# The first eight heads of an attention and feed-forward kernel: bias rows by products, wide exps, and casts on another engine

## The chip, the cores and the metric

The kernel runs on one core of one Trainium2 chip. A core has a matrix engine (TensorE, PE in the profile, with PEld for its weight loads), VectorE (DVE), ScalarE (ACT), GpSimd (POOL) and SyncE (SP). Each works through its own instructions in order, and semaphores let one wait for another. SP and POOL issue the DMA transfers of this kernel. SBUF holds the tiles; PSUM holds the results of products in 8 banks, each 128 partitions by 512 fp32 values. The metric is device time in microseconds (us), lower is better.

## The reference

Eight batches of eight heads, 576 positions of 64 values each, go through causal attention with a bias from running sums, and the result goes through a gated feed-forward block:

```python
scores = scale * np.matmul(q, k.transpose(0, 1, 3, 2))          # scale = 1/8
cum = np.cumsum(np.maximum(s, 0.0), axis=-1)
bias = -(cum[:, :, :, None] - cum[:, :, None, :])
scores = np.where(causal, -1e9, scores + np.minimum(bias, 0.0))
attn = softmax(scores)                                          # over the last axis
x = np.matmul(attn, v)  # (B, H, S, D) -> (B*S, H*D): 4608 x 512
out = (silu(x @ w_gate) * (x @ w_val)) @ w_out                  # 512 -> 1536 -> 512
```

Below the diagonal the bias is never positive, so the minimum needs no work of its own.

## The kernel before

Heads are handled in blocks of four (`hb`, 16 blocks; blocks 0 and 1 are batch 0). For a block, k and q are loaded as fp32 (`load_one`, L136), cast to bf16 (`cast_half` L248, `cast_one` L239), and transposed, for the early blocks by products with an identity on PE (`pe_transpose_half` L292, `pe_transpose` L281) into PSUM. `pe_out` (L305) copies the transposed halves out of PSUM into the tile `KQ`, nine groups of 128 columns in pieces of five and four, the upper and the lower 64 partitions into two tiles.

A tile `KQ[i][r]` holds 64 partitions of transposed q and k of two heads, and 64 partitions of bias rows, of which four are in use: the running sum split into a bf16 high and low part on one side (k or q), and constants 1 and -1 on the other. A product over all 128 partitions thus gives scores and bias together. The rest of the bias rows must be zero. The running sums are made by DVE into the tile `HL` (L200 to L232), one partition per head, and `aug` (L178) brings each head's four rows to its `KQ` tile with one small DMA per head.

`score_piece` (L338) makes the scores of one head in four pieces of at most 512 columns, each in one PSUM bank; two of them begin with a product that adds the causal mask (`lower`), in batch 0 only. ACT takes exp of each piece into the tile `pt`. So a head has three exps of 512 columns and one of 64. `av_piece` multiplies `pt` with v and a column of ones, `av_out` divides by the sum, `x_pe` (L439) transposes the result into `XT`, and the feed-forward block works from `XT` in tiles of 512 positions.

PSUM banks are handed out in Python by `take`, which takes the one that was given back first, and `give`. All order is written by hand: what stands first in the function is issued first on its engine. L905 to L976 are the opening that the change concerns: block 0 cast in halves by ACT and POOL, its transposes and bias rows, block 1 cast by DVE (L921), v of batch 0 cast by POOL (L924), the loads issued by POOL (v at L914, weights at L915 and L928, further k and q), the scores of heads 0 to 3 with block 1's transposes between them (`half_batch`, L891), heads 4 to 7, and `values`. `keep_warm` (L881) is products whose result nobody uses. After L976 the feed-forward work of one tile and the attention of the next batches are interleaved by a position counter (`pump`).

Of the kernel before, what the change touches and what calls it, by code (L numbers as in the profile page):

```python
# [19 lines left out]
def kernel(  # L20
# [11 lines left out]
    nc = tc.nc  # L32
# [73 lines left out]
    c8 = first.tile([BH, S], FP32)  # L106
    PTP = {0: first, "bufs": 7}
    lower = first.tile([128, 512], BF16)

    with tc.manual_schedule():  # L110
# [4 lines left out]
        bank = {i: psb.tile([128, 512], FP32, name=f"bank{i}") for i in range(8)}  # L115
# [4 lines left out]
        def take():  # L120
            b = min(bank, key=lambda x: released[x])
            assert released[b] < OPEN
            released[b] = OPEN
            return b
# [8 lines left out]
        def view16(b, w):  # L133
            return bank[b][:, 0 : w // 2].bitcast(BF16)
# [43 lines left out]
        def aug(hb, engs):  # L178
            for hh in range(HB):
                r, e = divmod(hh, 2)  # L180
                r0 = 64 * (1 - r)
                bh = hb * HB + hh
                engs[hh].dma_start(  # L183
                    KQ[hb % 2][r][r0 : r0 + 4, :, e * S : (e + 1) * S],
                    HL[bh : bh + 1, :, :, :],
                )
# [12 lines left out]
        nc.scalar.activation(warm, warm, AF.Exp)  # L199
        nc.vector.memset(HL[:, 0:2, 0, :].bitcast(FP32), ONES2)  # L200
# [6 lines left out]
        )  # L207

# [4 lines left out]
        for r in range(2):  # L213
            nc.gpsimd.memset(aug_rows(0, r)[:, 1, :], 0.0)
            nc.scalar.mul(
                KQ[0][r][64 * (1 - r) : 64 * (1 - r) + 64, 0, :],
                one_s[0:64, 0:1].to_broadcast([64, NR * S + 64]), 0.0,
            )
        pads(0)
        nc.vector.memset(aug_rows(1, 0), 0.0)  # L220
        for nm in ("k", "q"):
            load_one(1, nm, eng=nc.gpsimd)
        init_vt(0)
        pads(1)
# [67 lines left out]
        def pe_transpose_half(hb, name, g, r):  # L292
            j0, j1 = JG[g]
            if r == 0:
                bs = take()
                ps = view16(bs, (j1 - j0) * 128).rearrange("p (j x) -> p j x", x=128)
                tps[name, g] = [ps, bs, 2]
            ps = tps[name, g][0]
            ct = cts[name, hb]
            for j in range(j0, j1):  # L300
                nc.tensor.transpose(
                    ps[64 * r : 64 * r + 64, j - j0, :], ct[:, j, r, :], ident
                )
# [575 lines left out]
        spare = take()  # L879
# [5 lines left out]
        def row_half(nm, r, eng):  # L885
            for g in range(2):
                pe_transpose_half(0, nm, g, r)
            for g in range(2):
                pe_out(0, nm, g, r, eng)

        def half_batch(nm):  # L891
            for g in range(2):
                pe_transpose(1, nm, g)
                pe_out(1, nm, g, 0, nc.vector)

        def scores(h):
            for ci in range(4):
                score_piece(h, ci)
# [9 lines left out]
        aug(0, SP4)  # L908
        row_half("k", 0, nc.scalar)
        row_half("q", 0, nc.vector)  # L910
        cast_half(0, "k", 1, nc.scalar)
        cast_half(0, "q", 1, nc.gpsimd)
        nc.gpsimd.memset(aug_rows(1, 1), 0.0)
        load_v(0, range(5), nc.gpsimd)  # L914
        w_load("g", 0)  # L915
        aug(1, SP4)
        keep_warm(10)
        row_half("k", 1, nc.scalar)
        row_half("q", 1, nc.vector)
        keep_warm(10)  # L920
        cast_one(1, "k", nc.vector)  # L921
        cast_one(1, "q", nc.vector)
# [10 lines left out]
        scores(0)  # L933
        half_batch("k")
        scores(1)
        half_batch("q")
        scores(2)
        scores(3)
        for nm in ("k", "q"):
            for g in range(2):  # L940
                pe_out(1, nm, g, 1, nc.vector)
# [34 lines left out]
        give(spare)  # L976
# [88 lines left out]
```

## Time and profile before

| What | us |
|---|---|
| median of 3 runs | 375.78 (375.11 to 376.01) |
| the profiled execution | 375.79 |
| its span | 374.0 |
| PE busy | 360.7 |
| DVE busy | 289.6 |
| ACT busy | 240.4 |
| POOL busy | 212.3 |

The span runs from the first to the last instruction of one profiled execution, and all starts below count from its beginning. A row of the timeline has start, length, engine, line, operation, written tile <- read tiles, shapes, count, and in brackets the idle time of the engine ahead of it with what ended it. A row of the chain of waits has start, length and what the end waited for at that time. A group has busy time and mean length of one (ns). The granted TensorE clock was 0.999 in this execution.

### The profile page before, as it was taken

What the parts mean: (1) busy time and instruction counts of PE and PEld (TensorE: products, weight loads), DVE (VectorE), ACT (ScalarE), POOL (GpSimd) and SP (SyncE); (2) the same over time, 40 slices, a digit from 0 to 9 for tenths busy, and PEclk for the clock granted to TensorE, in tenths of its full rate; (3) what the DMA queues carried; (4) which work ended last, traced back from release to release, by engine and by line L of the source; (5) the groups of instructions that cost most, each with busy time, mean ns of one, the idle gap of its engine ahead of it and who ended that gap; (6) DMA issues with size and microseconds to landing.
All of it is one profiled execution on the core that took longest, in us unless ns stands there. A gap on an engine that the chain in (4) does not pass through costs nothing.

```text
span 374.0 us, 8759 instructions
## 1 busy us (share of the span) xinstructions
PE 360.7 (96%) x3259; PEld 230.6 (62%) x3300; DVE 289.6 (77%) x578; ACT 240.4 (64%) x471; POOL 212.3 (57%) x325
## 2 busy tenths in 40 slices
PE   7799899999999999999999999999999999999995
PEld 6584456655555556855685559655865585476464
DVE  8968776468995899588967997699858867975984
ACT  8777677698876877588757875686566523323321
POOL 8883555856455647494649464955675516315320
PEclk9999999999999999999999999999999999999999
DMA  7899999799877997896779675984132103002003
GB/s 239 193 258 253 219 257 267 237 303 247 245 186 220 254 262 196 178 281 205 211 167 266 178 182 174 255 206 98 40 119 62 35 19 128 2 0 95 20 0 114
DMA packets 97146, 64.23 MB, mean 172 GB/s; under 512 B 77232, under 2 KB 82736, under 8 KB 97104
## 3 DMA queue, kind: packets, MB, share of 16 engines
q1 hardware_dynamic: 84976, 41.46, 45.2%
q0 software_dynamic: 12128, 22.21, 22.6%
q8 instruction: 26, 0.43, 0.5%
q14 instruction: 16, 0.13, 0.1%
HBM read 37.90 MB, written 19.86 MB: 154 GB/s over the span
## 4 chain that ended last, share of the span: by engine, by line
PE 85%; DMA 6%; POOL 5%; ACT 1%; issue 1%; DVE 1%; DVEq 0%; POOLq 0%; ACTq 0%
PE bank L629 45%; PE bank L735 17%; PE bank L359 10%; PE bank L396 7%; PE bank L686 5%; DMA rawk<-in_k_dram 4%; DMA rawv<-in_v_dram 2%; POOL rawv L157 1%; POOL vt L168 1%; POOL wv L332 1%; ACT pt L369 1%; PE bank L287 0%; POOL rawq L140 0%; ACT kq L314 0%; POOL kq L211 0%
## 5 line engine op out<-in xcount | busy, mean ns | idle before, releaser
L369 ACT ACTIVATE pt<-bank 128x512 bf16<-128x512 f32 (+1 forms) x256 | 120.4, 510 | 31.0 <-PE bank L359 18.2
L629 PE MATMUL bank<-XT,wg 128*128 128x512 bf16 x418 | 110.3, 379 | 1.2 <-DVE pp L652 0.3
L629 PE MATMUL bank<-XT,wv 128*128 128x512 bf16 x412 | 109.3, 379 | 1.1
L650 ACT ACTIVATE th<-bank 128x512 bf16<-128x512 f32 x108 | 64.7, 599 | 55.9 <-PE bank L629 53.6
L652 DVE SCALAR_TENSOR_TENSOR pp<-th,bank 128x512 bf16<-128x512 bf16 x108 | 73.6, 682 | 19.2 <-ACT th L650 18.7
L663 DVE SCALAR_TENSOR_TENSOR ht<-pp,bank 128x512 bf16<-128x512 bf16 x108 | 74.1, 686 | 10.6 <-PE bank L629 0.4
L359 PE MATMUL bank<-kq 128*128 128x128 bf16 (+4 forms) x576 | 75.6, 240 | 1.5 <-DMA kq<-HL 1.0
L672 POOL TENSOR_TENSOR ht<-ht 128x512 bf16<-128x512 bf16 x35 | 40.4, 1154 | 52.2 <-DVE su L670 52.1
L359 PEld LDWEIGHTS <-kq 128*128 128x128 bf16 x576 | 45.8, 98 | 31.5 <-issue 1.9
L629 PEld LDWEIGHTS <-wv 128*128 128x128 bf16 x432 | 38.4, 98 | 36.5 <-issue 0.6
L629 PEld LDWEIGHTS <-wg 128*128 128x128 bf16 x432 | 38.3, 98 | 34.2 <-issue 0.7
L396 PEld LDWEIGHTS <-pt 128*128 128x128 bf16 x960 | 41.9, 98 | 17.2
L374 POOL TENSOR_SCALAR_AFFINE_SELECT pt<-pt 128x512 bf16<-128x512 bf16 x56 | 36.8, 658 | 27.3 <-ACT pt L369 22.7
L396 PE MATMUL bank<-vt,pt 128*128 128x65 bf16 x960 | 47.0, 194 | 0.4 <-POOL vt L168 0.3
L430 POOL DMA_DIRECT2D xs<-ot x24 | 21.7, 905 | 30.0 <-DVE ot L413 27.6
L735 PEld LDWEIGHTS <-ht 128*128 128x128 bf16 x336 | 31.2, 98 | 4.3
L413 DVE TENSOR_TENSOR ot<-bank,rc 128x320 bf16<-128x320 f32 x64 | 31.5, 492 | 2.2
L183 POOL DMA_DIRECT2D kq<-HL x48 | 28.9, 604 | 0.0
L735 PEld LDWEIGHTS <-su 128*128 128x128 bf16 x252 | 23.5, 98 | 3.3
L686 PE MATMUL bank<-wo,ht 128*128 128x512 bf16 x90 | 24.8, 379 | 0.3
L800 POOL TENSOR_TENSOR ysb<-ysb 128x512 f32<-128x512 f32 x12 | 15.2, 1270 | 15.3 <-DVE ysb L794 15.3
L379 POOL TENSOR_SCALAR_AFFINE_SELECT pt<-pt 128x64 bf16<-128x64 bf16 x56 | 14.8, 264 | 15.8 <-ACT pt L369 15.7
(93 smaller groups left out, 384.6 us busy)
## 6 DMA issues: line engine op xcount, KB each, us to landing
out_dram<-ysb POOLq DMA_DIRECT2D x32, 256.0 KB, 4.5
rawv<-in_v_dram SPq DMA_DIRECT2D x28, 256.0 KB
rawk<-in_k_dram SPq DMA_DIRECT2D x12, 576.0 KB
rawq<-in_q_dram SPq DMA_DIRECT2D x12, 576.0 KB
xs<-ot POOLq DMA_DIRECT2D x24, 160.0 KB, 3.5
ks<-ck SPq DMA_DIRECT2D x11, 288.0 KB
qs<-cq SPq DMA_DIRECT2D x11, 288.0 KB
rawk<-in_k_dram POOLq DMA_DIRECT2D x3, 576.0 KB, 7.3
```

The lines of the kernel that those rows point to most:

```text
L359: nc.tensor.matmul(sc[:, o : o + w], T[:, 1, e * S + 128 * tj : e * S + 128 * (tj + 1)], T[:, 0, e * S + lo : e * S + hi], start=not maske ...
L369: nc.scalar.activation(pt[:, c0 : c0 + n], sc, AF.Exp, scale=0.125)
L374: nc.gpsimd.affine_select(pt[:, 1088:1600], pt[:, 1088:1600], pattern=[[0, 4], [1, 128]], compare_op=ALU.is_ge, fill=zreg, base=0, channel ...
L396: nc.tensor.matmul(av[:, bi * (D + 1) : (bi + 1) * (D + 1)], pt[:, c0 : c0 + 128], VT[b % 2][:, tj, h, :], start=(tj == 0), stop=(tj == bi),)
L413: nc.vector.tensor_mul(ot[:, :, e * D : (e + 1) * D], av3[:, :, 0:D], rc[:, :, None].to_broadcast([128, NCH, D]),)
L629: nc.tensor.matmul(view(bs, TT), w[:, c, f0 : f0 + 128], xt[:, c, :], start=(c == 0), stop=(c == 3),)
L650: nc.scalar.activation(th, pg, AF.Tanh, scale=0.5)
L652: nc.vector.scalar_tensor_tensor(pp, in0=th, scalar=1.0, in1=pg, op0=ALU.add, op1=ALU.mult)
L663: nc.vector.scalar_tensor_tensor(hp[:, 2 * k2 : 2 * k2 + 2, :].rearrange("p a n -> p (a n)"), in0=pp, scalar=0.5, in1=pv, op0=ALU.mult, op ...
L672: (nc.vector if ft == NFT - 1 else nc.gpsimd).tensor_sub(hp[:, 1:3, :], hp[:, 1:4:2, :], hp[:, 0:3:2, :])
L686: nc.tensor.matmul(view(pys[ts_], DM), hps[ft // 2][:, 2 * (ft % 2) + half, c0 : c0 + 128], WO[j][:, ft % WKO, :], start=(ft == 0), stop=( ...
L735: nc.tensor.matmul(ps, lhs(p), rhs(p), start=(first and p == 0), stop=(last and p == NP - 1), skip_group_check=True,)
```

## The change

The eight banks become one PSUM tile, so that an instruction can cover two adjacent banks. For heads 0 and 1 the bias rows no longer come by DMA: a selection matrix (`sel`) in a product with `HL` puts the head's high and low part of the running sum on the right partitions of a pair of banks (`pick`), and ACT or DVE turns that into the k row and the q row with a scale and an offset per partition (`picked_row`). Heads 2 to 7 keep their DMAs. In batch 0, `wide_scores` makes a head's scores in two parts over a pair of banks, with exps of 1024 and 576 columns. The early transposes go to banks 0 to 2, which are kept for them, and each copy out covers nine groups (`early_out`), or four on ACT and five on DVE. The casts of block 0's second half (k) and of block 1 (k and q) go to POOL; the first load of v is issued ahead of them. Memsets are spread differently, and `keep_warm` has fewer products.

```diff
+    sel = first.tile([BH, 2, 2, 128], BF16)
...
-        bank = {i: psb.tile([128, 512], FP32, name=f"bank{i}") for i in range(8)}
+        banks = psb.tile([128, 8, 512], FP32, name="banks")
+        bank = {i: banks[:, i, :] for i in range(8)}
...
+        def take_pair():
+            b = min(range(7), key=lambda x: max(released[x], released[x + 1]))
+            assert max(released[b], released[b + 1]) < OPEN
+            released[b] = released[b + 1] = OPEN
             return b
...
+        for h in range(2):
+            for lo in range(2):
+                nc.vector.tensor_copy(
+                    sel[:, h, lo, 64 + lo : 68 : 2], ident[0:BH, h : h + 1].to_broadcast([BH, 2])
+                )
...
+        def early_transpose(hb, name, r=None):
             ct = cts[name, hb]
+            ps = early(name, 0, J)
+            for j in range(J):
+                if r is None:
+                    nc.tensor.transpose(ps[:, j, :], ct[:, j].rearrange("x r d -> x (r d)"), ident)
+                else:
+                    nc.tensor.transpose(ps[64 * r : 64 * r + 64, j, :], ct[:, j, r, :], ident)
...
+        for i in range(3):
+            released[i] = OPEN
+        spare = 7
...
+        def pick(h):
+            b = picked[h] = take_pair()
+            for lo in range(2):
+                for c0, c1 in ((0, 512), (512, S)):
+                    nc.tensor.matmul(
+                        banks[:, b + c0 // 512, 0 : c1 - c0], sel[:, h, lo, :],
+                        HL[:, lo, 1, c0:c1], start=(lo == 0), stop=(lo == 1),
...
+            if eng is nc.scalar:
+                nc.scalar.activation(dst, src_t, AF.Identity, bias=c[up, 0:1], scale=a[up, 0:1])
+            else:
+                eng.tensor_scalar(dst, src_t, a[up, :], c[up, :], ALU.mult, ALU.add)
...
+            b = take_pair()
+            order = ((1, 0), (2, 3))[part]
...
+            c0, n = CHUNK_PT[order[0]], (1024, 576)[part]
+            nc.scalar.activation(
+                pt[:, c0 : c0 + n],
+                banks.rearrange("p b n -> p (b n)")[:, b * 512 : b * 512 + n],
+                AF.Exp, scale=0.125,
+            )
...
-        aug(0, SP4)
-        row_half("k", 0, nc.scalar)
-        row_half("q", 0, nc.vector)
-        cast_half(0, "k", 1, nc.scalar)
+        aug(0, SP4, (2, 3))
+        aug(1, SP4)
+        early_transpose(0, "k", 0)
+        early_out(0, "k", 0, nc.scalar)
+        early_transpose(0, "q", 0)
+        pick(0)
+        load_v(0, range(1), nc.gpsimd)
+        cast_half(0, "k", 1, nc.gpsimd)
+        picked_row(0, 1, nc.scalar)
+        picked_row(0, 0, nc.vector)
+        picked_done(0)
+        early_out(0, "q", 0, nc.scalar, 0, 4)
+        early_out(0, "q", 0, nc.vector, 4, J)
+        pick(1)
+        early_transpose(0, "k", 1)
         cast_half(0, "q", 1, nc.gpsimd)
-        nc.gpsimd.memset(aug_rows(1, 1), 0.0)
-        load_v(0, range(5), nc.gpsimd)
+        for c in range(1, 5):
+            load_v(0, range(c, c + 1), nc.gpsimd)
+        picked_row(1, 1, nc.vector)
+        picked_row(1, 0, nc.vector)
+        picked_done(1)
+        keep_warm(4)
+        give(spare)
         w_load("g", 0)
-        aug(1, SP4)
-        keep_warm(10)
-        row_half("k", 1, nc.scalar)
-        row_half("q", 1, nc.vector)
-        keep_warm(10)
-        cast_one(1, "k", nc.vector)
-        cast_one(1, "q", nc.vector)
+        init_vt(0)
+        cast_one(1, "k", nc.gpsimd)
+        cast_one(1, "q", nc.gpsimd)
+        scores(0)
+        early_transpose(0, "q", 1)
+        early_out(0, "k", 1, nc.vector)
+        early_out(0, "q", 1, nc.scalar, 0, 4)
+        early_out(0, "q", 1, nc.vector, 4, J)
...
-        scores(0)
-        half_batch("k")
         scores(1)
-        half_batch("q")
-        scores(2)
+        early_transpose(1, "k")
+        early_out(1, "k", 0, nc.vector)
+        wide_scores(2, 0)
+        early_transpose(1, "q")
+        early_out(1, "q", 0, nc.scalar, 0, 4)
+        early_out(1, "q", 0, nc.vector, 4, J)
+        wide_scores(2, 1)
         scores(3)
-        for nm in ("k", "q"):
-            for g in range(2):
-                pe_out(1, nm, g, 1, nc.vector)
+        early_out(1, "k", 1, nc.vector)
+        early_out(1, "q", 1, nc.vector)
```

## The prediction

> **What bounds the kernel now.** The page comes first, for the size of the thing, then its chain of waits, to see which stretch is not plain TensorE work:
>
> ```profile
> span 374.0 us, 8759 instructions
> PE 360.7 (96%) x3259; PEld 230.6 (62%) x3300; DVE 289.6 (77%) x578; ACT 240.4 (64%) x471; POOL 212.3 (57%) x325
> PE 85%; DMA 6%; POOL 5%; ACT 1%; issue 1%; DVE 1%; DVEq 0%; POOLq 0%; ACTq 0%
> ...
> 22.81 15.78 DMA rawk<-in_k_dram
> 38.72 1.15 POOL ck L246
> ```
>
> PE carries the chain, and what is not PE lies ahead of 40 us: POOL's issues, then one load of k (head block 3) issued at 22.81 and landed at 38.60. The change touches only the work ahead of about 25 us, so I read that stretch in the timeline:
>
> ```profile
> 10.91 0.83 PE L359 MATMUL bank<-kq 128*128 128x128 bf16 x8 [0.99 <-DMA kq<-HL]
> 11.34 13.53 ACT L369 ACTIVATE pt<-bank 128x512 bf16<-128x512 f32 x32 [1.63 <-PE bank L359]
> 19.53 1.27 PE L396 MATMUL bank<-vt,pt 128*128 128x65 bf16 x30
> 23.42 0.44 PE L445 MATMUL bank<-ident,ot 128*128 128x128 bf16 x5
> 33.39 1.57 ACT L369 ACTIVATE pt<-bank 128x512 bf16<-128x512 f32 x3 [0.27 <-ACT th L650]
> 39.92 0.45 PE L287 MATMUL bank<-ident,ck 128*128 128x128 bf16 x5 [1.16 <-POOL ck L246]
> ...
> 9.51 4.89 POOL L157 DMA_DIRECT2D rawv<-in_v_dram x5
> 14.39 0.78 POOL L332 DMA_DIRECT2D wg<-in_moe_w_gate_dram x1
> 10.56 0.76 DVE L246 CAST ck<-rawk 128x1152 bf16<-128x1152 f32 x1
> 11.24 1.12 DVE L246 CAST cq<-rawq 128x1152 bf16<-128x1152 f32 x1
> 24.94 1.14 POOL L246 CAST ck<-rawk 128x1152 bf16<-128x1152 f32 x1 [1.36 <-DMA rawk<-in_k_dram]
> ```
>
> Head 0's scores wait at 10.91 for the bias row's DMA. Then 32 exps run almost without a hole, 1.69 us a head. Values of head 0 begin at 19.53, right after head 5's scores; the first transposes of attention output begin at 23.42. From there PE is packed (4.00 of 4.00 us busy in 28 to 32) until it idles 1.16 us for block 3's k. That wait is the only slack: work before it may come 1.16 us later for nothing, anything beyond goes into the end, since after 56 us no PE wait reaches the listing's threshold.
>
> Prices come from the groups by form:
>
> ```profile
> L369 ACT ACTIVATE pt<-bank 128x512 bf16<-128x512 f32 x24 | 12.6, 622 | 1.9 <-PE bank L359 1.6
> L369 ACT ACTIVATE pt<-bank 128x64 bf16<-128x64 f32 x8 | 2.2, 272 | 0.0
> L316 DVE COPY kq<-bank 64x640 bf16<-64x640 bf16 x7 | 5.7, 817 | 1.0 <-PE bank L287 0.7 <-PE bank L301 0.3
> L316 DVE COPY kq<-bank 64x512 bf16<-64x512 bf16 x7 | 5.0, 712 | 0.0
> L450 ACT COPY XT<-bank 128x576 bf16<-128x576 bf16 x2 | 1.3, 638 | 1.2 <-PE bank L445 1.2
> ```
>
> **The change, part by part.**
>
> *Wide exps.* A column costs (622-272)/448 = 0.78 ns, and three 512s in 1.57 us with the last at 0.60 make one step 0.485. So 1024 columns step in 0.90 (1.02 to the end) and 576 in 0.55 (0.67): 1.45 a head against some 1.6 now, 1.2 us over eight heads at most. Bounds of a head: 1.26 (columns alone) and 1.69 (today's pace). [...]
>
> *Head 0's rows.* ACT's two zeroings and two casts stand as now, and the nine k transposes end at 6.09. The copy of all nine, 64x1152 on ACT: 640 took 0.75, 512 took 0.72, 1216 from SBUF 1.21; I take 1.16, so 6.15 to 7.3. The ninth q transpose lies in that copy's bank and waits for it, and the picks are queued behind it on PE: one transpose (0.06), products of 512, 64, 512, 64 columns (0.216 a 512, from four in 1.03 with the last 0.38) and a tail of 0.2 end at 8.05. A product lies between 0.19 (64 columns) and 0.38. The added DVE work (memset, four tiny copies, three scalars: eight at 0.06, a memset, to 0.19, a reciprocal, so 0.5 to 1.5 us, less the removed 1.07 us memset) costs nothing: the bias low part ends at 6.83 now, and the picks wait until 7.36. Without that cover it would cost at most 0.4.
>
> From the picked pair ACT makes the k row, 64x576 (0.638 for XT's 576; bounds 0.6 and 1.21): 8.1 to 8.75. DVE's q row waits for ACT, as both read one pair: 0.72 (0.553 for a 576 scale in SBUF, 0.751 for two inputs), 8.8 to 9.55. DVE's half of the q copy waits for ACT's half (9.35) and follows, 0.82: 10.4. The k transposes of heads 2 and 3 wait for that copy on PE, and head 0's scores are queued behind them: 0.5, plus four warm products 0.25. Scores begin at 11.25, against 10.91. The DMA wait went; ACT, DVE and PE in a row took its place.
>
> [...]
>
> [...]
>
> *Heads 0 and 1.* A head's first part is 1536 columns, 0.65 and a tail, and its exp needs all of it: first exp at 12.1 (now 11.34). Exps: 12.1 to 13.0 and 13.0 to 13.55. Second part waits for DVE's rows of head 1 (two of 0.72 after 10.4: 11.85). Head 1's first part takes the same pair of banks and waits for the first exp's end, 13.15; ready 14.0. ACT copies half of q in between (0.58): exps 14.15 to 15.6.
>
> *The casts of block 1 move from DVE to POOL*, behind more of POOL's queue. Now they end at 12.36. On POOL: from 2.6, a 64x1216 memset 1.05, five small ones at 0.33, issues of k, q and the first v chunk 0.91+0.78+0.92, two half casts at 0.64, four v issues from 10.42 to 14.39 now, 3.97, wg 0.77, vt's memsets 0.8, the casts 1.14 each. Running sum: 5.3, 7.95, 9.2, 13.2, 14.0, 14.8; casts end at 15.9 and 17.05. With every memset at 0.20 and every v issue at 0.70 it is 14.0 and 15.1; I keep the rows' means. Head 2's scores are queued on PE behind the k transposes of block 1: 15.9, 0.5, first part 16.4, exp at 17.2. ACT stands idle from 15.6.
>
> *Heads 2 to 5.* The q transposes' ninth waits for DVE's 64x1152 copy (0.712+640*0.82 ns = 1.24; bounds 0.82 and 1.53), 17.85; second part 18.0, ready 18.4. ACT: exp 17.2, q half copy 18.1, exp 18.7 to 19.25. Head 3's first part, after the first exp of head 2 (18.2): 18.3, exp 19.25. Head 4, on the same pair again, after 20.3: exp 21.2. Head 5's lies where the transposes were and waits for two more 1.24 copies behind a 0.8 on DVE: 18.95+0.8+2.48 = 22.25. Its scores end at 23.2.
>
> *To 23.42.* Now 3.89 us pass from the start of the values (19.53) to 23.42, on PE alone; I keep them. Values begin at 23.2, so the transposes at 27.1: **3.7 us late**.
>
> *After it.* All to 38.76 is fed by PE and shifts. Block 3's k lands no later: POOL issues it at some 24.3 instead of 22.81, but the same queue is then still working off weights (landings from 28.29 to 37.05), and POOL's cast, behind selects that wait for ACT, ends before PE comes at 42.4. So 1.16 is swallowed. Removed (two 9 KB bias transfers, warm products): nothing, other transfers and other waits cover them.
>
> Sum: +3.7 - 1.16 = +2.5. The profiled execution took 375.79 (span 374.0 and 1.8 around it), beside a median of 375.78: **378.3**.
>
> **Rivals.**
> 1. *The front hangs on DMA, and the change helps DMA (the other side).* The DMA engines are 45% busy in 10 to 12 us, as v's first issue comes at 9.51; the first v chunk now goes out at 7. That may pull the stream, and block 3's k, 1.0 us forward, 1.5 at most (all that is lost from 10 to 14). Then the time is 375.8 minus 1.0 to 1.5, 374.3 to 374.8, but only if the transposes of 23.42 come no later than they do now; each us later takes one off. Against it: the casts at 15.9.
> 2. *POOL is quicker (14.0 and 15.1).* Then DVE's copy of the k half sets head 2 (15.2), and all is 0.7 to 2 us nearer: +0.5 to +1.8, 376.3 to 377.6.
> 3. *The v loads of batch 1 come too late.* SP issues them after head 7's scores, 24.54 now, some 28.2 then, and the k and q loads stand behind them. If bandwidth doesn't make that good, POOL's 1.45 us wait for q at 56.88 reaches PE: 379.5 to 381.
>
> **How the numbers follow.** Forecast 0.56, with 377.6 to 379.3 of its own from the memset, copy and exp bounds; rival 1 0.18, partly spent, so half of it ends within 0.3% (1.1 us, about what this kernel's timing can tell from none); rival 2 0.16; rival 3 0.10. Faster 0.09; within 0.3% 0.12 (0.09 from rival 1, 0.03 from rival 2); slower 0.79. The range 375.7 to 379.9 leaves out some 0.12 below and 0.06 above.
>
> **What would show it.** First exp near 12.1; POOL's casts of block 1 ending near 16 and 17; an ACT hole of over 1 us before head 2; five-transpose groups starting near 27 instead of 23.42; no PE wait for block 3's k. It is wrong if POOL's casts end before 14.5, if the DVE copies of 1152 cost 0.8, or if the 27.1 is right and the end doesn't follow.

## The result, and the profile after

The changed kernel takes 380.72 us (median of 4 executions, 379.48 to 381.29), the kernel before on the same chip 375.75 (375.11 to 376.01). The ratio is 1.0116, with a 95% interval of 1.0077 to 1.0155. The forecast was 378.3 with a range to 379.9: the direction was right, the loss twice as large as forecast. The profiled execution took 379.48, the shortest of the four. In some executions of most kernels, of the one before too, the time is 2.5 to 3.5 us longer than in the rest, so times below are medians.

The page of the changed kernel, its first lines and its shares of the chain:

```profile
span 377.8 us, 8763 instructions
...
PE 364.7 (97%) x3292; PEld 231.4 (61%) x3292; DVE 290.3 (77%) x581; ACT 240.3 (64%) x455; POOL 213.4 (56%) x327
...
PE 87%; DVE 6%; ACT 3%; issue 1%; DMA 1%; POOL 1%; DVEq 0%; SPq 0%; ACTq 0%
```

The span grew by 3.8. PE's busy time is 4.0 higher, but that tells little: in the profile before, 41 of the 3300 products (as many as there are weight loads) have no record, here none of 3292 is missing, and a kernel below whose clock held has 364.6 too. In the chain DVE has 6% where it had 1%, and DMA 1% where it had 6%. So waits for transfers left the chain, and DVE's work took their place.

The timeline of the changed kernel (start, length, engine, line, operation, and in brackets the idle time before it with what ended it):

```profile
8.60 0.83 ACT L937 ACTIVATE kq<-banks,r_m,r_k 64x576 bf16<-64x576 f32 x1 [0.90 <-PE banks L926]
9.46 0.89 DVE L939 TENSOR_SCALAR kq<-banks,r_q,r_k 64x576 bf16<-64x576 f32 x1 [1.61 <-ACT kq L937]
10.38 0.82 DVE L335 COPY kq<-banks 64x640 bf16<-64x640 bf16 x1
11.25 0.66 PE L325 MATMUL banks<-ident,ck 128*64 128x128 bf16 x9 [2.20 <-DVE kq L335]
13.19 1.56 ACT L975 ACTIVATE pt<-banks 128x1024 bf16<-128x1024 f32 x2 [3.02 <-PE banks L967]
13.94 1.14 POOL L267 CAST ck<-rawk 128x1152 bf16<-128x1152 f32 x1
15.03 1.15 POOL L267 CAST cq<-rawq 128x1152 bf16<-128x1152 f32 x1
16.98 0.66 PE L323 MATMUL banks<-ident,ck 128*128 128x128 bf16 x9 [0.59 <-DVE kq L335]
18.34 1.02 ACT L975 ACTIVATE pt<-banks 128x1024 bf16<-128x1024 f32 x1 [0.62 <-PE banks L967]
...
24.47 1.08 PE L428 MATMUL banks<-vt,pt 128*128 128x65 bf16 x30
...
28.17 0.44 PE L477 MATMUL banks<-ident,ot 128*128 128x128 bf16 x5
...
43.74 0.44 PE L308 MATMUL banks<-ident,ck 128*128 128x128 bf16 x5
```

ACT, DVE, DVE and PE follow each other from 8.60 to 11.25, as forecast. The first exp starts at 13.19 (before: 11.34), the values at 24.47 (19.53), the x transposes at 28.17 (23.42): 4.75 late. The products of block 3's k start at 43.74 with no wait, where before they started at 39.92 after a wait of 1.16, so 3.82 are left there. The span is longer by the same 3.8, so on the whole nothing of it is won back or lost later.

What is not in the forecast stands in the windows of the changed kernel (stretch in us; busy us and instructions of each engine; granted PE clock; DMA share; GB/s):

```profile
core 0: us, PE busy (x) PEld busy (x) DVE busy (x) ACT busy (x) POOL busy (x), PEclk, DMA share, GB/s
...
10.00:12.00 2.00, 0.75 (x12) 0.65 (x12) 1.94 (x3) 0.17 (x1) 2.00 (x3) 1.00 0.90 254
12.00:14.00 2.00, 2.00 (x19) 1.57 (x18) 0.92 (x2) 0.81 (x1) 1.88 (x5) 0.63 1.06 254
14.00:16.00 2.00, 2.00 (x16) 1.33 (x15) 1.17 (x1) 1.48 (x3) 2.00 (x2) 0.52 0.99 168
16.00:18.00 2.00, 1.41 (x20) 1.06 (x18) 1.25 (x3) 1.56 (x2) 1.76 (x4) 1.00 1.14 188
```

After PE's idle time of 2.20 us up to 11.25 the granted clock is halved, by the trace from 12.50 to 15.91. Just then PE makes the scores of heads 0 and 1 and transposes q, and it is busy all the time. The kernel before holds 1.00 there.

### The profile page after: what moved, and what is told of

Read it like the earlier page. It is cut to its first block, busy times and chain, and to the rows that moved or that the text cites. A ratio compares the mean times of both kernels' runs of the same rounds, so it can differ in the third digit from the quotient of the medians.

```text
span 377.8 us, 8763 instructions
## 1 busy us (share of the span) xinstructions
PE 364.7 (97%) x3292; PEld 231.4 (61%) x3292; DVE 290.3 (77%) x581; ACT 240.3 (64%) x455; POOL 213.4 (56%) x327
## 4 chain that ended last, share of the span: by engine, by line
PE 87%; DVE 6%; ACT 3%; issue 1%; DMA 1%; POOL 1%; DVEq 0%; SPq 0%; ACTq 0%
PE banks L661 45%; PE banks L767 17%; PE banks L391 9%; PE banks L428 7%; PE banks L718 5%; DVE kq L335 2%; DVE pp L684 1%; DVE ht L695 1%; DVE kq L348 1%; PE banks L967 1%; DMA rawk<-in_k_dram 1%; ACT pt L401 1%; PE banks L325 1%; POOL vt L179 1%; PE banks L477 1%
## 5 line engine op out<-in xcount | busy, mean ns | idle before, releaser
L401 ACT ACTIVATE pt<-banks 128x512 bf16<-128x512 f32 x224 | 107.0, 506 | 28.1 <-PE banks L391 15.6
L661 PE MATMUL banks<-XT,wg 128*128 128x512 bf16 x432 | 111.5, 379 | 0.5 <-DVE pp L684 0.3
L661 PE MATMUL banks<-XT,wv 128*128 128x512 bf16 x432 | 110.9, 379 | 0.2 <-DVE pp L684 0.2
L682 ACT ACTIVATE th<-banks 128x512 bf16<-128x512 f32 x108 | 64.7, 599 | 56.2 <-PE banks L661 50.2
L684 DVE SCALAR_TENSOR_TENSOR pp<-th,banks 128x512 bf16<-128x512 bf16 x108 | 73.6, 682 | 18.4 <-ACT th L682 18.1
L695 DVE SCALAR_TENSOR_TENSOR ht<-pp,banks 128x512 bf16<-128x512 bf16 x108 | 74.1, 686 | 12.1 <-PE banks L661 0.8
L391 PE MATMUL banks<-kq 128*128 128x128 bf16 (+4 forms) x504 | 68.3, 240 | 0.7 <-DVE kq L348 0.3
L428 PE MATMUL banks<-vt,pt 128*128 128x65 bf16 x960 | 46.8, 194 | 0.3 <-POOL vt L179 0.3
L445 DVE TENSOR_TENSOR ot<-banks,rc 128x320 bf16<-128x320 f32 x64 | 31.5, 492 | 2.2
L718 PE MATMUL banks<-wo,ht 128*128 128x512 bf16 x96 | 25.8, 379 | 0.0
```

Source lines behind the costliest of these rows:

```text
L391: nc.tensor.matmul(sc[:, o : o + w], T[:, 1, e * S + 128 * tj : e * S + 128 * (tj + 1)], T[:, 0, e * S + lo : e * S + hi], start=not maske ...
L401: nc.scalar.activation(pt[:, c0 : c0 + n], sc, AF.Exp, scale=0.125)
L428: nc.tensor.matmul(av[:, bi * (D + 1) : (bi + 1) * (D + 1)], pt[:, c0 : c0 + 128], VT[b % 2][:, tj, h, :], start=(tj == 0), stop=(tj == bi),)
L445: nc.vector.tensor_mul(ot[:, :, e * D : (e + 1) * D], av3[:, :, 0:D], rc[:, :, None].to_broadcast([128, NCH, D]),)
L661: nc.tensor.matmul(view(bs, TT), w[:, c, f0 : f0 + 128], xt[:, c, :], start=(c == 0), stop=(c == 3),)
L682: nc.scalar.activation(th, pg, AF.Tanh, scale=0.5)
```

## The experiments

Each kernel ran beside the kernel before on the same chip, whose medians were 375.49 to 376.33; a ratio is to its executions, and isn't one of medians. Line numbers shift by a few where an edit adds or removes lines. The profiled executions of `e12_apart`, `e14_k_cast` and `e15_head2_first` (379.92, 379.88 and 379.57) lie some 3 us above the medians of these kernels, so starts in them say nothing of the usual execution, and these kernels are judged by their medians.

### Is it the clock?

`e1_warm`, 36 warm products in PE's idle time after head 1's picks:

```diff
         pick(1)
+        keep_warm(36)
         early_transpose(0, "k", 1)
```

> The changed kernel with 36 more warm products between the picks and the k transposes of heads 2 and 3, where PE stood idle for 2.20 us and the granted clock then fell to 0.50 from 12.2 to 15.5 us. Theory A (the opening's lateness is a chain over PE, DVE and ACT, and the halved clock is one link of it): clock 1.0 throughout, first exp near 12.8 instead of 13.19, the k transposes of block 1 near 16.0 instead of 16.98, the x transposes near 27.2 instead of 28.2, time 379.7 against 380.7. Theory B (the clock is no link, DVE's copies alone set it): clock 1.0 but block 1's transposes stay at 16.98, time 380.7. Theory C (the half clock is the main cost): 377.5 or less.

Four executions fell into two groups, 378.80 and 379.02 at a mean clock of 1.000, 382.01 and 382.16 at 0.991 and 0.996; ratio 1.0126 (1.0073 to 1.0179). In the profiled one (379.02) the clock is 1.00 throughout, the first exp is at 12.65, and the x transposes start at 27.12, against 27.1 in the forecast. So at full clock the x transposes come when the forecast has them. The two shorter times lie between theory A (379.7) and theory C (377.5 or less): the clock is a link of the chain, and a larger one than theory A had. The two longer ones may be executions in which the clock was down when the 36 products ran, which then take 4 us and push the scores; the run `e9_apart` below shows such a case, for these two it is only argued.

That is too many products, so `e17_warm16` has 16 in the same place, and `e18_after_again` is the changed kernel once more, on the same chip and with more executions:

> The changed kernel with 16 warm products after head 1's picks (1 us of TensorE's 2.2 us of idleness there). If the products hold the clock: the granted clock at 1.00 in most executions, x transposes at 27.0 to 27.6, time 378.3 to 379.2 in the lower group, with one execution in four or five 2.5 to 3 us above it, where the first q block lands late. If 1 us of the 2.2 is not enough: the clock falls as in the changed kernel, x transposes at 28.0 to 28.5, time 379.5 to 381.

> The changed kernel itself, again, for more executions. If the missing warm products are the rest of the loss, most executions show a mean clock below 0.998 and the median stays at 380 to 381; if it was a chance of few executions, most executions lie at 378.5 to 379.5 with a few at 380.5 to 382.

Measured: 378.65 with the 16 products (12 executions, 378.12 to 379.27; ratio 1.0061, 1.0043 to 1.0080), 380.45 without (6 executions, 379.66 to 380.81; ratio 1.0102, 1.0071 to 1.0132). Five of the six without have mean clocks of 0.990 to 0.995, eleven of the twelve with have 0.998 to 1.000. The late group that I had expected of the 16 products, one execution in four or five, did not show. The sixth execution without has a clock of 1.000 and a span of 376.7, as long as those with the products (376.4 to 377.5), where the other five have 378.4 to 379.1; its time, 379.66, lies 3.0 above its span, where the others lie 1.7 to 2.1 above. The second trace of the changed kernel has the clock at 0.50 from 10.1 to 17.0; its x transposes start at 29.09. Two of its windows:

```profile
10.00:12.00 2.00, 0.86 (x9) 0.86 (x8) 1.94 (x4) 0.05 (x1) 2.00 (x3) 0.53 0.92 270
12.00:14.00 2.00, 2.00 (x15) 1.33 (x14) 0.81 (x2) 0.00 (x0) 1.91 (x4) 0.50 1.04 232
```

The timeline of the kernel with 16 products:

```profile
9.03 1.07 PE L918 MATMUL banks<-ident 128*128 128x128 bf16 x16
...
11.30 0.66 PE L325 MATMUL banks<-ident,ck 128*64 128x128 bf16 x9 [1.20 <-DVE kq L335]
...
12.98 1.56 ACT L975 ACTIVATE pt<-banks 128x1024 bf16<-128x1024 f32 x2 [2.77 <-DVE kq L939]
...
16.27 0.66 PE L323 MATMUL banks<-ident,ck 128*128 128x128 bf16 x9 [1.12 <-POOL cq L267]
...
17.63 1.02 ACT L975 ACTIVATE pt<-banks 128x1024 bf16<-128x1024 f32 x1 [0.74 <-PE banks L967]
...
27.46 0.44 PE L477 MATMUL banks<-ident,ot 128*128 128x128 bf16 x5
```

and its windows:

```profile
12.00:14.00 2.00, 1.93 (x24) 1.42 (x23) 0.96 (x2) 1.02 (x2) 1.90 (x4) 1.00 0.98 238
14.00:16.00 2.00, 1.15 (x13) 0.88 (x12) 1.89 (x2) 1.95 (x4) 1.98 (x2) 1.00 1.09 187
```

The products end long before PE is needed at 11.30 and delay nothing. With them PE is busy for 3.08 of the 4 us from 12 to 16 and has its waits back, where it was busy for all 4.00, and 1.80 us of the time are gone. That is the price of the missing warm products.

One thing stands against reading the clock off these means alone: of the first four executions of the changed kernel, one took 380.82 with a mean of 1.000. A mean of 1.000 doesn't rule out a slow opening. The profiled execution of `e14_k_cast` below has 1.000 too, and its windows read 1.00 from 4 to 30 us, but products of its opening are slow:

```profile
6.46 0.67 ACT L275 CAST cq<-rawq 128x576 bf16<-128x576 f32 x1 [1.38 <-DMA rawq<-in_q_dram]
...
7.18 1.17 PE L325 MATMUL banks<-ident,cq 128*64 128x128 bf16 x9 [0.88 <-ACT cq L275]
```

Nine transposes take 1.17 there, as long as in `e9_apart` below, where the clock is 0.53 from 12 to 16 (1.17 at 14.43), and 0.66 with 1.00 in the windows (11.30 above). Whether the 380.82 was such an execution can't be told, as it has no trace.

`e8_cold` is the test from the other side, the kernel before without its 20:

```diff
-        keep_warm(10)
         row_half("k", 1, nc.scalar)
         row_half("q", 1, nc.vector)
-        keep_warm(10)
```

> The kernel before without its 20 warm products (two groups of ten, between the transposes of batch 0's first block and its first scores); nothing else is changed and the result is the same. Theory A (the products keep the granted clock; that was the step costed at nothing): TensorE's busy share from 7.5 to 11.5 us falls from 0.66 to about 0.36, the granted clock falls to 0.50 for one stretch of about 3.4 us, the scores of heads 0 and 1 take twice as long, and the x transposes come at 24.5 to 25.5 instead of 23.42; of that the wait of 1.16 us for block 3's k at 39 us takes back most, so the end moves by 0 to +0.8 (375.8 to 376.6). Theory B (the products are fill, and the fall of the clock in the changed kernel comes from its 2.2 us of idle TensorE alone): the clock stays at 1.00, x transposes within 0.3 of 23.42, the time 375.5 to 376.0.

Measured: 376.36 (375.68 to 377.21), ratio 1.0019 (1.0003 to 1.0034). Its windows, and then its timeline:

```profile
12.00:14.00 2.00, 2.00 (x20) 1.68 (x18) 1.32 (x3) 1.59 (x4) 2.00 (x3) 0.53 0.74 213
14.00:16.00 2.00, 2.00 (x20) 1.52 (x19) 0.74 (x2) 1.68 (x4) 1.87 (x3) 0.62 0.89 236
```

```profile
11.90 1.69 ACT L369 ACTIVATE pt<-bank 128x512 bf16<-128x512 f32 x4 [2.08 <-PE bank L359]
...
21.24 1.08 PE L396 MATMUL bank<-vt,pt 128*128 128x65 bf16 x30
...
25.13 0.44 PE L445 MATMUL bank<-ident,ot 128*128 128x128 bf16 x5
```

The clock falls there too, to 0.50 from 12.1 to 15.5, and the x transposes come 1.71 late, nearly as much as the 1.63 between the profiled runs with and without products above (29.09 and 27.46). But the span is longer by 0.4 only (374.4), because the wait for block 3's k is gone. So theory A holds in both parts. In the kernel before the products look nearly free to remove, since the slack covers them; in the changed kernel the other delays had spent that slack already (with 16 products PE doesn't wait for block 3's k either), and the whole 1.8 showed.

### Are the rows, the exps or the slack to blame?

`e2_dma_rows`, the rows of heads 0 and 1 by DMA again, 24 warm products ahead of head 0's scores, and a memset of head 0's rows on DVE:

```diff
-        aug(0, SP4, (2, 3))
+        aug(0, SP4)
...
-        pick(0)
...
-        picked_row(0, 1, nc.scalar)
-        picked_row(0, 0, nc.vector)
-        picked_done(0)
...
-        keep_warm(4)
+        keep_warm(24)
```

> The changed kernel with the bias rows of heads 0 and 1 brought by DMA again; wide exps, nine-group copies and POOL casts stay, and 24 warm products stand before head 0's scores. Theory A (picked rows put ACT, DVE and PE in a row): k transposes of heads 2 and 3 near 9.4 instead of 11.25, head 0's scores near 11.4 when the DMA lands, first exp near 12.3, block 1's transposes near 15.4, x transposes 1.6 earlier, time 379.1. Rival (the rows are no part of the loss; wide exps on two pairs of banks and DVE copies make it): 380.7.

Measured: 381.48 (380.11 to 382.05), ratio 1.0140 (1.0101 to 1.0179). Its timeline:

```profile
8.59 23.32 SPq L194 DMA_DIRECT2D kq<-HL  x16
...
13.80 0.61 PE L967 MATMUL banks<-kq 128*128 128x448 bf16 x2 [0.66 <-DMA kq<-HL]
15.10 1.57 ACT L975 ACTIVATE pt<-banks 128x1024 bf16<-128x1024 f32 x2 [7.37 <-PE banks L967]
```

Head 0's row is issued at 8.59 and frees PE at 13.80, 5.2 us later; in the kernel before it was 7.51 to 10.90, 3.4. The DMA engines are 0.94 and 0.99 busy from 8 to 14 here, and were 0.74 busy from 8 to 11 there. Head 0's scores begin there at 13.80, in the changed kernel at 12.08, so in this arrangement, with v's first chunk out early, the rows by DMA come later than picked rows. Neither time that I had expected (379.1 or 380.7) came, and what the rows are worth isn't shown: the running sums came 0.65 later (the memset; the first row is issued at 8.59 instead of 7.94), and the clock was 0.50 from 7.9 to 14.7.

`e3_narrow`, the changed kernel with four exps a head:

```diff
-            for part in range(2):
-                wide_scores(h, part)
+            for ci in range(4):
+                score_piece(h, ci)
```

> The changed kernel with each head's scores in four pieces of one bank and four exps again; all else stays. Theory A (a pair of banks is refilled only after its whole exp, which costs more than the fewer exps save): first exp 0.4 earlier, time 379.9 to 380.4. Rival (wide exps save ACT 1.2 us on the way to the end, as by the count of columns): 381.9.

Measured: 380.68 (380.14 to 381.11), ratio 1.0130 (1.0100 to 1.0161), beside 380.45 and 380.72 of the changed kernel. The time is that of the changed kernel, neither theory A's nor the rival's. The four exps take 1.69 a head and follow the scores, so they look covered either way; that the clock was at 0.50 here from 9.1 to 16.0, for 6.8 us where the changed kernel has 3.41, leaves room for a few tenths.

`e5_k3_early`, the kernel before with the load of block 3's k ahead of two weight loads:

```diff
+        load_one(3, "k", eng=nc.gpsimd)
         for nm in ("g", "v"):
             w_load(nm, 1, 0)
-        load_one(3, "k", eng=nc.gpsimd)
```

> The kernel before, with the load of block 3's k issued ahead of the two halves of the second weight blocks instead of behind them. Theory A (PE's 1.16 us wait for that k at 38.76 is slack that nothing else fills): the wait goes and the time falls by 1.1, to 374.6. Rival (the weights, or another transfer, are late next and take its place): 375.7 or more.

Measured: 375.53 (375.10 to 378.83), ratio 1.0003 (0.9974 to 1.0032). The wait for block 3's k is gone; in the profiled execution the x transposes came 0.81 late at 24.23, and block 3's products at 39.41 instead of 39.92. A gain in the median did not show within the interval. That the wait absorbs lateness is shown by all other runs: between ACT's fifth and sixth tanh in the feed-forward work (37.56 and 41.30 in the kernel before) each comes 1.32 or 1.33 nearer to the kernel before.

### What holds the rest of the opening

With 16 warm products 2.4 us remain (378.65 against 376.28 of the kernel before in the same runs). The next kernels take one hold after another off the changed kernel. `e9_apart`: q and k in two early banks each, instead of three banks that share one, with 36 warm products. `e10_act_copy`: the last q copy of block 1 on ACT, with 36 warm products. `e11_both`: both, and one of head 1's rows on ACT.

```diff
-            c0 = SRC[name][1] * J * 128
+            c0 = SRC[name][1] * 2048
...
-        for i in range(3):
+        for i in range(4):
             released[i] = OPEN
...
-        picked_row(1, 1, nc.vector)
+        picked_row(1, 1, nc.scalar)
...
-        early_out(1, "q", 1, nc.vector)
+        early_out(1, "q", 1, nc.scalar)
```

> The changed kernel with 36 warm products after head 1's picks (as in the run before of that name), and with the early transposes of q and k in two banks each instead of three banks together. Theory A (the shared bank and the wait for DVE's copies hold the opening): the ninth q transpose no longer waits for ACT's copy (7.47), picks start by 7.3, the first exp comes 0.3 earlier (12.3), block 1's k transposes start when DVE's k copy ends (15.15) and not at 15.94, heads 2 to 5 follow 0.5 to 1.0 earlier, x transposes at 26.2 to 26.6 instead of 27.12, the end 0.5 to 0.9 under that run's: 378.1 to 378.5 in an execution at full clock. Theory B (DVE's six copies and the exps, in a row, set heads 2 to 5, whatever the banks): x transposes at 26.8 to 27.1, the time within 0.3 of that run's.

> The changed kernel with the 36 warm products, and with the last copy of block 1's q (64x1152, 1.35 us on DVE) put on ACT. Theory A (head 5's scores wait for two whole copies in a row on DVE, 19.80 to 22.44): they start at 21.2 to 22.0 instead of 22.5, values at 22.4 instead of 23.42, x transposes at 26.2 to 26.5, the end 0.6 to 0.9 under the run with warm products alone. Theory B (ACT is the bound there: 1.1 us more on it delay head 4's exps by 0.75 and all after them): x transposes at 27.0 to 27.5, the time within 0.4 of that run's.

> The changed kernel with the warm products, q and k in banks of their own, the last q copy on ACT, and one of head 1's two rows on ACT instead of DVE (0.89 us there, in the 2.7 us in which ACT stands idle before the first exp). If the opening is held by the banks and DVE's queue, the three add up: first exp at 12.0 to 12.3, x transposes at 25.0 to 25.8 instead of 27.12, the end 1.3 to 2.0 under the run with warm products alone, 377 to 377.6. If ACT's exps (heads 0 to 5, 1.57 each with their steps) or the transfers are the next bound, less than 0.8 of it is seen.

Two of the three failed by their own construction: `e9_apart` 382.32 (380.79 to 383.06), `e11_both` 381.91 (380.46 to 382.25). The timeline of `e9_apart` says why; `e11_both` has the same wait of 1.8 us, and a clock of 0.81 in 8 to 12 and 0.77 in 12 to 16:

```profile
9.43 1.11 PE L926 MATMUL banks<-HL,sel 64*128 64x512 bf16 x4 [1.84 <-DVE kq L939]
...
10.48 4.02 PE L918 MATMUL banks<-ident 128*128 128x128 bf16 x36
```

With one bank kept for the warm products only three were left, two overlapping pairs, so head 1's picks waited 1.84 for DVE's row of head 0. The clock fell (0.62 in 8 to 12, 0.53 in 12 to 16), and the 36 products took 4.02 us, where they took 2.18 in `e1_warm` at 1.00, with the scores queued behind them. Warm products were cheap here only where they ended before the next work was ready.

`e10_act_copy` took 378.07 (377.95 to 379.63), ratio 1.0065 (1.0041 to 1.0090). Its x transposes start at 27.18, so theory B holds there: ACT's 1.11 us delays the exps by what DVE's queue no longer does. Its time is under the two shorter ones of `e1_warm` all the same, by 0.8; two holes of PE later on (0.55 at 29 to 30 us and 0.40 between the fourth and the fifth tanh, 39.66 and 42.32) are in that run's profile and not in this one's, and I don't know their cause. The second is in the changed kernel's profile too.

`e12_apart` mends `e9_apart`: the warm products write into the unused end of the fourth early bank, no bank is held back, and there are 16 of them. `e13_all` is that with the last q copy and one row of head 1 on ACT.

> The changed kernel with q and k in two early banks each, the warm products (16 after head 1's picks instead of 36) written into the unused end of the fourth of these banks, and no bank held back for them, so that head 1's picks have two banks of their own beside head 0's. In the run with separate banks before this, the picks of head 1 waited 1.84 us for DVE's row of head 0, since two pairs of three banks overlap, the clock fell to 0.50 and 36 products took 4 us. Theory A (the shared bank and the wait for DVE's copies hold the opening): no such wait, first exp at 11.8 to 12.4 (changed kernel 13.19), block 1's k transposes follow DVE's k copy directly, x transposes at 25.5 to 26.6 (changed kernel 28.17, with 36 warm products 27.12), the end 377 to 378.3. Theory B (DVE's copies in a row and ACT's exps set heads 2 to 5): x transposes at 26.7 to 27.2, the end 378.3 to 379. If the clock falls nevertheless, about 1.5 us more.

> As the run before in this list, and the last q copy of block 1 and one of head 1's rows on ACT instead of DVE. Theory A: first exp at 11.3 to 12.0, x transposes at 24.6 to 25.6, the end 375.8 to 377.2, level with the kernel before at best, because 1.33 us of the opening's lateness is taken back by the wait for block 3's k that goes. Theory B (ACT is the next bound, by the copy's 1.11 us): x transposes within 0.4 of the run before in this list.

Measured: 377.15 (377.01 to 379.92), ratio 1.0047 (1.0021 to 1.0073), and 377.53 (376.86 to 380.18), ratio 1.0049 (1.0022 to 1.0075). Banks of their own are worth some 1.5 us against the 16 products alone, by medians, so the shared bank was a hold (theory A). Six of the ten executions of `e12_apart` lie at 377.01 to 377.17, under all twelve with the products alone; by the ratios, in which its three executions above 379 tell too, it is 0.5, and the intervals overlap. Moving the two further pieces to ACT adds nothing to that in the time, as theory B has it; but in four of the eight executions of `e13_all` the mean clock is 0.991 to 0.995, and its x transposes (26.83) have nothing to be set beside. The profiled execution of `e12_apart` took 379.92. Its timeline shows ACT's second cast waiting for the first load of q, with the clock down after that:

```profile
6.80 0.67 ACT L275 CAST cq<-rawq 128x576 bf16<-128x576 f32 x1 [1.72 <-DMA rawq<-in_q_dram]
```

In `e14_k_cast` and `e15_head2_first` that cast starts at 6.46 and 6.43, in the other profiles of these kernels at 5.3 to 5.9. In `e14_k_cast` the nine transposes after it took 1.17 (7.18, above), in the other two the clock was at 0.50 from 7.6 or 8.1 to 14.5 or 15.0. So in these three long executions a late first load of q and a slow opening go together.

In `e13_all` the first exp is at 11.07, even before the 11.34 of the kernel before, and then something else holds the opening. Its timeline:

```profile
14.02 1.14 POOL L267 CAST ck<-rawk 128x1152 bf16<-128x1152 f32 x1
...
15.22 0.68 PE L323 MATMUL banks<-ident,ck 128*128 128x128 bf16 x9 [1.97 <-POOL ck L267]
...
16.59 1.02 ACT L973 ACTIVATE pt<-banks 128x1024 bf16<-128x1024 f32 x1 [1.62 <-PE banks L965]
```

Here PE waits 1.97 us for POOL's cast, with head 2's scores behind it, and the clock falls after it (0.65 and 0.50 in 16 to 20, so 0.50 from 16.6 to 20.0). That is the hold which the forecast had put into the changed kernel. So `e14_k_cast` moves the cast of k to DVE, and `e15_head2_first` puts head 2's first scores ahead of block 1's k transposes:

```diff
-        cast_one(1, "k", nc.gpsimd)
         cast_one(1, "q", nc.gpsimd)
...
         early_out(0, "k", 1, nc.vector)
+        cast_one(1, "k", nc.vector)
```

> As the run of all three moves before it, and the cast of block 1's k (1.14 us on GpSimd, ending there at 15.1) on VectorE, in the 1.05 us in which VectorE waits between its copies of block 0's k and q; GpSimd then casts only q, from 14.0 to 15.2. In the run of all three moves TensorE waited 1.97 us for that cast (to 15.22) and the clock then fell to 0.50 from 16 to 19.4. Theory A (GpSimd's casts of block 1 hold head 2 as soon as the opening is early enough, which is the place that the prediction had given them in the changed kernel too early): TensorE's block-1 k transposes at 14.2 to 14.5, head 2's first exp at 14.9 to 15.4 instead of 16.59, the clock at 1.00, x transposes at 24.9 to 25.7 instead of 26.83, the end 1.0 to 1.9 earlier than in that run, in time 375.0 to 376.2, level with the kernel before. Theory B (ACT's exps and copies, or the cast of q, take its place at once): x transposes within 0.5 of 26.83, time 376.5 to 377.5.

> As the run before in this list, with head 2's first two scores ahead of block 1's k transposes in TensorE's order, instead of behind them. If the transposes' waits still hold head 2, its first exp comes at 14.9 and the following ones without a hole, and x transposes 0.3 to 0.6 earlier than in the run before in this list; if heads 4 and 5 are bound by the copies of block 1 (k transposes, copy of 1.35, q transposes, copy of 0.82, scores), the k transposes now come 0.5 later and so do heads 4 and 5: x transposes 0 to 0.5 later.

Measured: 376.65 (376.06 to 379.88), ratio 1.0025 (0.9998 to 1.0052), and 376.89 (376.28 to 380.06), ratio 1.0046 (1.0023 to 1.0070). By medians and by ratios the cast is worth 0.9, a little less than forecast, but the intervals overlap, the kernel before was itself 0.7 quicker on this chip than beside `e13_all`, and 376.65 lies in theory B's range. So what the cast is worth isn't shown. The order of head 2 is worth nothing here, with the copies behind it the same.

`e16_dve_halves` is `e14_k_cast` with the q halves taken off ACT, one whole copy each on DVE; `e19_head2_first` is that with head 2 first; `e20_no_act_copy` is that with the last q copy back on DVE:

```diff
-        early_out(0, "q", 1, nc.scalar, 0, 4)
-        early_out(0, "q", 1, nc.vector, 4, J)
+        early_out(0, "q", 1, nc.vector)
...
+        wide_scores(2, 0)
         early_transpose(1, "k")
         early_out(1, "k", 0, nc.vector)
-        wide_scores(2, 0)
```

> As the run with the k cast on VectorE, with the two halves of q that ACT copies between the exps of heads 1 and 2, and of heads 2 and 3 (0.72 each), moved into one whole copy each on VectorE (1.35 instead of 0.82). If ACT is the bound of heads 1 to 5 there, head 2's first exp follows head 1's last, heads 4 and 5 come 0.7 to 1.5 earlier, x transposes at 23.6 to 24.8, and the time is 374.8 to 376, under or level with the kernel before. If VectorE's copies (1.36, 1.35, cast 0.98, 1.36, 1.35 in a row) take ACT's place, x transposes come within 0.5 of that run's when it isn't disturbed (25.4), time 376.2 to 377.

> As the run with whole q copies on VectorE, with head 2's first scores ahead of block 1's k transposes in TensorE's order. In that run these transposes waited 1.3 us for VectorE's cast, with head 2's scores behind them. If that order holds heads 2 and 3: head 2's first exp at 14.4 to 14.8 instead of 15.93, head 4's at 18.6 to 19.2 instead of 20.59 (behind ACT's copy), x transposes at 23.6 to 24.4 instead of 25.51, the time 374.8 to 375.7, under the kernel before. If heads 4 and 5 are bound by the copies of block 1 on VectorE (15.28 to 17.9): head 4 at 18.3 at the earliest, and x transposes at 24.4 to 25.2, time 375.7 to 376.4.

> As the run before in this list, with the last q copy of block 1 (64x1152) back on VectorE (1.35) instead of ACT (1.11). If ACT's copy delays heads 4 and 5 (it lies between the exps of heads 3 and 4), head 4's exp comes 0.3 to 1.1 earlier and x transposes 0.3 to 1.0 earlier, time 0.3 to 0.9 lower; if head 6 then waits for that copy on VectorE (its end at about 20.6), nothing is gained, within 0.3.

Measured: 376.54 (376.12 to 380.00), ratio 1.0016 (0.9992 to 1.0041); 376.35 (375.72 to 376.70), ratio 1.0010 (0.9991 to 1.0028); 376.26 (376.00 to 381.34), ratio 1.0027 (0.9995 to 1.0058). The timeline of `e19_head2_first`:

```profile
11.19 1.57 ACT L973 ACTIVATE pt<-banks 128x1024 bf16<-128x1024 f32 x2 [1.08 <-PE banks L965]
...
15.05 1.02 ACT L973 ACTIVATE pt<-banks 128x1024 bf16<-128x1024 f32 x1 [0.36 <-PE banks L965]
...
15.56 4.00 DVE L335 COPY kq<-banks 64x1152 bf16<-64x1152 bf16 x3 [1.01 <-PE banks L323]
...
24.89 0.44 PE L477 MATMUL banks<-ident,ot 128*128 128x128 bf16 x5
```

The first exp and head 2 come early, and then DVE copies block 1 for 4.00 us in a row, with ACT's copy between the exps of heads 3 and 4 (18.84, 1.11 us). So the second reading of each expectation was right: the x transposes reach 24.9, not 24.4. That is 1.47 behind the kernel before, and the wait for block 3's k absorbs 1.33. The kernel is level with the one before, by an interval that holds 1 and reaches to 1.0 us above it. None of these versions beats it.

## Why the prediction was wrong

*The step that failed* is "Removed (two 9 KB bias transfers, warm products): nothing, other transfers and other waits cover them". For the warm products it cost 1.8 us (380.45 against 378.65). Cover was the wrong question to ask of them: they do no work that could be covered; what they do is keep PE's clock up for the work that follows (with 16 of them it is 1.00 in all windows of `e17_warm16`, without them 0.50 from 10.1 to 17.0 in `e18_after_again`). I had the rows for it: the clock of 1.00 in all stretches before, and my own steps left PE nothing but head 1's picks between 8.05 and DVE's copy at 10.4. With this one term in place, the forecast stands at 380.1, and without the clock's fall the kernel takes 378.65 where 378.3 was forecast. That the rest agrees so well is in part luck: the rows for heads 0 and 1 cost more than I took, POOL's casts less, and what held head 2 was not what I had named.

*Head 0's rows.* The chain was right: ACT, DVE, DVE, PE in turns, as forecast, in place of the DMA. DVE's row waited 1.61 us for ACT's, which ended at 9.43, and started at 9.46. That it has to wait, as both read one pair of banks, and what the turns cost, no run shows. With 16 products its scores begin at 12.12 instead of 11.25. ACT's copy of nine starts 0.48 later than I had it (6.63), and both rows were under-sized: 0.83 on ACT for the 0.64 taken, 0.89 on DVE for 0.72. The groups by form of the changed kernel (busy us, mean ns, idle before):

```profile
L975 ACT ACTIVATE pt<-banks 128x1024 bf16<-128x1024 f32 x8 | 8.2, 1023 | 5.8 <-PE banks L967 5.5 <-ACT pt L975 0.3
L335 DVE COPY kq<-banks 64x1152 bf16<-64x1152 bf16 x4 | 5.3, 1356 | 2.7 <-PE banks L325 1.9 <-PE banks L323 0.8
L975 ACT ACTIVATE pt<-banks 128x576 bf16<-128x576 f32 x8 | 5.2, 647 | 0.0
L333 ACT COPY kq<-banks 64x1152 bf16<-64x1152 bf16 x1 | 1.1, 1112 | 0.1
L937 ACT ACTIVATE kq<-banks,r_m,r_k 64x576 bf16<-64x576 f32 x1 | 0.8, 826 | 0.9 <-PE banks L926 0.9
```

The k row has a scale and an offset per partition, and costs 826, 188 ns more than the 638 of a plain 576-column copy (of 128 partitions, from bf16). How much of the 188 is due to the two operands, no run shows.

*Wide exps.* 1.02 and 0.65 were taken as 1.02 and 0.67 (by its own rate the bound of 1.26 a head is 1.25, and nothing rests on it). `e3_narrow`, with four exps a head, takes the same time, so they seem to stay off the path.

*The casts of block 1 on POOL.* They end at 15.08 and 16.18, between my bounds, 0.8 before the value that I took; 0.66 of it is the four issues of v ahead of them, 3.31 for 3.97. In the changed kernel they did not hold head 2: DVE's copies of block 0, which freed the shared banks at 16.93, did. That is what rival 2 had said of the mechanism, though not of its time, as the rows were later too. With the clock held, both end within 0.04 us of each other (16.21 and 16.25). The cast became the hold that I had described once the copies were out of its way (`e13_all`, 1.97 us). So the term was a second hold right behind the first, not the bound.

*Heads 2 to 5.* A copy of 1152 columns on DVE costs 1.36 where 1.24 was taken. The x transposes start at 27.46 with 16 products and at 27.12 with 36, where 27.1 was forecast; of the late first exp (0.9) half was swallowed ahead of head 2, whose first exp starts at 17.63 for 17.2.

*The slack.* Swallowed as forecast, 1.33 instead of 1.16, when PE no longer waited for block 3's k. But 0.40 of new lateness came just ahead of it (ACT's fifth tanh is 5.14 late, the fourth 4.74), so only 0.93 of the 4.75 was won back; why, no run shows. Block 3's k lands at 35.68 instead of 38.60: the part of rival 1 which says that transfers come forward was right (the DMA share from 10 to 12 us rose from 0.45 to 0.90), but PE came later than the load, so it bought nothing. Rival 3, late loads of v, did not show: from 41 us to the end the distance to the kernel before stays between 3.8 and 4.2.

What stays open: the two longer executions of `e1_warm`, the two small later holes in its profile, and why the first load of q comes a microsecond late in some executions.

## What to carry to other kernels

Products whose result nobody uses are not free to remove: ask which work follows them, and how long PE is otherwise idle ahead of it (2.20 us in the changed kernel, 1.20 with the 16 products). If the clock may fall there, price that work at the low clock too: here the nine transposes took 1.17 for 0.66, and the 36 products 4.02 for 2.18. A removal tested alone may look free because slack elsewhere absorbs it (0.4 here), and cost its full price (1.8) in a change that has already used that slack. When one hold is taken away, the next one is often within a microsecond of it: list what each waiting instruction needs besides the last thing it waited for.

## What the runs showed of the hardware

PE's clock fell between 4 and 20 us in ten of the 19 profiled executions, in each of them once. In the trace of the changed kernel it was 0.50 from 12.50 to 15.91, for 3.41 us. In the others the length is worked out from the means of windows of 2 or 4 us: about 3.4 at 0.50 in `e8_cold`, `e11_both` and `e13_all`, about 6.8 in `e2_dma_rows`, `e3_narrow`, `e9_apart`, `e12_apart`, `e15_head2_first` and `e18_after_again`. In the other nine, `e14_k_cast` with its slow opening among them, the windows of this stretch read 1.00.

PE's idle time beside it: in the changed kernel 2.20 us up to 11.25, clock down at 12.50; in `e8_cold` 1.66 up to 11.47, down at 12.1; in `e13_all` 1.97 up to 15.22, down at 16.6; in `e15_head2_first` 1.33 up to 7.15, down at 8.1. But it stayed at 1.00 in `e5_k3_early`, where PE waited 1.8 us for head 0's row and was busy for 0.28 of the 2 us from 10 to 12, and in `e17_warm16` with 1.20 up to 11.30 and products before it. So the length of the idle time alone doesn't tell whether the clock falls, and no run shows what does. The mean clock was 0.998 to 1.000 in 11 of 12 executions of `e17_warm16`, and 0.990 to 0.995 in five of six of `e18_after_again`, which lacks these products and has 2.2 us of idle time.

A head's bias rows (9 KB), brought by a small DMA, took 3.4 us from their issue to the work that waited for them with the DMA engines 0.74 busy (the kernel before, 8 to 11 us), and 5.2 with them at 0.94 to 0.99 (`e2_dma_rows`, 8 to 14 us).
